# A pooled-attention and gated-MLP kernel: k's second half pooled into both partition halves, third unit's scores ahead of v's pooling, ten small matmuls left out

## The chip, the cores and the metric

One Trainium2 chip, one core. The metric is the device time of one execution in microseconds (us). Engines are called as in the profile: PE (TensorE matmuls), PEld (its weight loads), DVE (VectorE), ACT (ScalarE), POOL (GpSimd), SP (SyncE).

## What is computed

Attention over pooled keys and values, then a two-layer network with a cosine gate. Inputs are float32, the output is [4608, 512] float32.

```python
batch, n_heads, seq, head_dim = (8, 8, 576, 64)
pool = 8; Sp = S // pool            # 72
k_p = k.reshape(B, H, Sp, pool, D).mean(axis=3)
v_p = v.reshape(B, H, Sp, pool, D).mean(axis=3)
scores = (1 / sqrt(D)) * q @ k_p.T  # per batch and head: 576 x 72
attn = softmax(scores)
x = (attn @ v_p) -> [4608, 512]     # tokens x (heads, head_dim)
h = x @ w_in                        # w_in 512 x 2048
out = (h * cos(h)) @ w_out          # w_out 2048 x 512
```

## The kernel before

The 4608 tokens are worked through in nine chunks of 512 (`t` from 0 to 8). Each chunk goes up (lines 350 and 357 to 360: matmuls with `w_in`, a cosine on ACT, a product on DVE into `g_sb`) and down (line 363 or 369: matmuls with `w_out`). The attention of the next batch is threaded between a chunk's down matmuls at places written out by hand. Everything is ordered by hand (`manual_schedule`): each engine runs its instructions in the order in which the program issues them, and waits on semaphores where it needs another engine's or a DMA's result.

Batch 0 has nothing to hide behind. Its attention is a prologue (lines 401 to 544), and this is where the change is. It runs in this order.

- Ten matmuls of one column each (line 406) and nine `warm_up` matmuls of 128x512 on a constant (line 492) run on PE before any data is there.
- SP's queue fetches the first half of k and q of batch 0 (heads 0 to 3, line 416); POOL's queue fetches the second half of k (line 92), of q (line 437) and both halves of v (line 92), and then the weights `w_in` and `w_out` in many parts (lines 137 and 142), all one after another. ACT and DVE cast the first half of k and q to bf16 (`first_k`, `first_q`).
- `pool_k_pairs(b, bank, pj, ...)` pools k of one pair of heads on PE (line 184): nine accumulating matmuls, one for each row `t`, with k as the weights (128 rows, 64 columns) and the constant matrix `groups` as the moving operand (144 columns: 72 pooled positions for each of the pair's two heads). The result stands in PSUM on 64 partitions; its `put` casts it into `kk` for both halves of the partitions (line 189), for each half by a copy of its own. `kk` holds pooled k twice since q, once transposed, may stand on either half.
- `q_transpose_mm` transposes blocks of q on PE (line 236) and copies them into `qT` (line 237).
- `scores(b, u, pair)` computes the scores of a unit, here 256 tokens by 4 heads: four matmuls (line 259) and an exp on ACT into `ex` (line 269). Batch 0 has four such units, `us[0]` to `us[3]`, ordered by heads, so that units 0 and 1 need pairs 0 and 1 of k and q, units 2 and 3 pairs 2 and 3. (A rest of 64 tokens comes with a later batch.)
- `sums_mm` (line 288) sums the exponentials with matmuls against a constant; ACT turns the sums into reciprocals with Ln and Exp (lines 523, 524, 303, 304).
- `pool_v_mm(b, pair, j0, j1)` pools v (line 198): 18 matmuls of 64 rows and 128 columns; its `put` copies to `vz` on DVE (line 202).
- `values_mm` (line 297) multiplies exponentials with pooled v, and `x_mul` (line 311) multiplies by the reciprocal on DVE into `xT`, which the up matmuls (line 350) read. The first eight up matmuls need heads 0 to 3 alone (units 0 and 1); the next need units 2 and 3.

PSUM is eight banks of 512 float32 per partition: `banks` are three pairs (called `one`, `two`, `three` in the prologue) and `obanks` two single ones.

Of the kernel before, what the change touches and what calls it, by code (L numbers as in the profile page):

```python
# [19 lines left out]
def kernel(  # L20
# [9 lines left out]
    nc = tc.nc  # L30
    B, H, S, D = q.shape
    Sp = S // POOL
# [7 lines left out]
    ROW = S // 64  # L40
# [27 lines left out]
    kk = [wpool.tile([128, H, SpA], BF16, name=f"kk{i}") for i in range(3)]  # L68
# [8 lines left out]
    def own(b):  # L77
        return b % 2 if b else 2

    banks = [psum.tile([128, 2, 512], FP32, name=f"bank{i}") for i in range(3)]  # L80
    obanks = [psum.tile([128, 512], FP32, name=f"obank{i}") for i in range(2)]
# [4 lines left out]
    staged, flat = {}, {}  # L86

    def even_view(src, b, j0=0, j1=KCH):
        return src[b, 2 * j0:2 * j1].rearrange("(j a) (p t) d -> (a p) j (t d)", a=2, t=ROW)
# [64 lines left out]
    half = (slice(0, 64), slice(64, 128))  # L154

    def v_part(b):
        return vz[own(b)][:, :, 0:4:3, :]
# [19 lines left out]
            s = s.rearrange("p (j a) t d -> p j a t d", a=2)  # L177
            add(out=v_part(b)[:, h0 // 2:h1 // 2], in0=s[..., 0, :], in1=s[..., 1, :], op=ADD)  # L178

    def pool_k_pairs(b, bank, pj):  # L180

        ps = bank[half[0], 0:2 * Sp]
        for t in range(ROW):
            nc.tensor.matmul(ps, lhsT=staged["k", b][:, pj, t, :], rhs=groups[:, t].rearrange("p a n -> p (a n)"),
                             start=(t == 0), stop=(t == ROW - 1))

        def put(copy):
            for rows in half:
                copy(out=kk[own(b)][rows, 2 * pj:2 * pj + 2, 0:Sp], in_=ps.rearrange("p (a n) -> p a n", a=2))

        return put

    def pool_v_mm(b, pair, j0, j1):
        vb = staged["v", b]
        n = (j1 - j0) * D
        for t in range(ROW):
            for hp, rows in enumerate(half):
                nc.tensor.matmul(pair[:Sp, hp, 0:n], lhsT=groups[rows, t, hp, :], rhs=vb[rows, j0:j1, t, :],
                                 start=(t == 0), stop=(t == ROW - 1))

        def put():
            nc.vector.tensor_copy(out=v_part(b)[:, j0:j1],
                                  in_=pair[:Sp, :, 0:n].rearrange("p a (j d) -> p j a d", d=D))

        return put
# [24 lines left out]
    def q_transpose_mm(b, bank, g0, g1):  # L230

        if ("qT", b) not in att:
            qT_tile(b)
        ps = bank.bitcast(BF16)[:, 0:(g1 - g0) * 128].rearrange("p (g n) -> p g n", n=128)
        for g in range(g0, g1):
            nc.tensor.matmul(ps[:, g - g0, :], flat[b][:, g * 128:(g + 1) * 128], identity, is_transpose=True)
        return lambda copy: copy(out=att["qT", b][:, g0:g1, :], in_=ps)  # L237
# [6 lines left out]
    def scores(b, u, pair):  # L244
        scores_mm(b, u, pair)
        scores_exp(b, u, pair)

    def scores_mm(b, u, pair):
        (c0, n), (h0, nh) = u

        for i in [i + 2 * a for k in range(0, nh, 4) for i in (k, k + 1) for a in range(2)]:
            bank, c = divmod(ex_col(u, i), nh * n // 2)
            pj, hp = divmod(h0 + i, 2)
            g, r = divmod(ROW * pj + ORDER[c0 // 64], 2)
            qT = att["qT", b]
            if (b, u) == (0, REST):
                (g, r), qT = divmod(pj, 2), att["qT", B - 1][:, QB:]
            ps = pair[bank][:Sp, c:c + n] if isinstance(pair, tuple) else pair[:Sp, bank, c:c + n]
            nc.tensor.matmul(ps.rearrange("p (g n) -> p g n", n=64),  # L259
                             lhsT=kk[own(b)][half[r], h0 + i, 0:Sp],  # L260
                             rhs=qT[half[r], g:g + n // 64, hp * 64:hp * 64 + 64])

    def scores_exp(b, u, pair):
        (c0, n), (h0, nh) = u
        ex = ex_rest[own(b)] if u == REST else asb.tile([Sp, 4 * 256], BF16, name="ex", tag="ex", bufs=EX)
        w = nh * n // 2
        for src, c, m in ([(pair[:Sp, :, 0:w], 0, 2)] if not isinstance(pair, tuple) else
                          [(bank[:Sp, 0:w].unsqueeze(1), a * w, 1) for a, bank in enumerate(pair)]):
            nc.scalar.activation(out=ex[:, c:c + m * w].rearrange("p (a n) -> p a n", a=m), in_=src,  # L269
                                 func=ACTF.Exp, scale=scale / POOL)  # L270
        att["ex", b, u] = ex
# [130 lines left out]
    kv_even_tiles(0)  # L402
    q_tile(0)
    one_of = nc.const_aps.tensor(1.0, [128, 1], BF16)
    for i in range(10):
        nc.tensor.matmul(obanks[0][0:1, 0:1], lhsT=one_of, rhs=one_of)
    nc.vector.memset(staged["q", 0][:, :, ROW - 1], 0.0)
    exp_tables()
    groups = consts.tile([128, ROW, 2, Sp], BF16, name="groups")
# [5 lines left out]
    for i, (src, n) in enumerate(((k, ROW * D), (q, (ROW - 1) * D))):  # L415
        nc.sync.dma_start(out=first[:, i].rearrange("p (j n) -> p j n", j=2)[:, :, 0:n],
                          in_=even_view(src, 0, 0, 2)[:, :, 0:n])
# [5 lines left out]
    def first_q(copy, j):  # L423
        n = ROW * D
        copy(out=staged["q", 0][:, j, 0:ROW - 1].rearrange("p t d -> p (t d)"), in_=first[:, 1, j * n:j * n + n - D])
# [4 lines left out]
    for rows in half:  # L430
# [7 lines left out]
                        in_=even_view(q, 0, 2, 4)[:, :, 0:(ROW - 1) * D])  # L438
# [50 lines left out]
    def warm_up(n, bank):  # L489

        for i in range(n):
            nc.tensor.matmul(bank, lhsT=one_of.to_broadcast([128, 128]), rhs=one_of.to_broadcast([128, 512]))

    vec, act = nc.vector.tensor_copy, nc.scalar.copy
    us = BY_HEADS
# [3 lines left out]

    one, two, three = banks  # L500
    warm_up(9, two[:, 0, :])
    puts = [pool_k_pairs(0, obanks[i], i) for i in range(2)]
    first_q(act, 0)
    first_q(vec, 1)
    puts[0](vec)
# [3 lines left out]
    warm_up(1, two[:, 0, :])  # L509
    scores(0, us[0], one)  # L510
    scores(0, us[1], two)
    puts = [pool_k_pairs(0, obanks[i], 2 + i) for i in range(2)]
    for put in puts:
        put(vec)
    s01 = one[:, 0, 256:512], two[:, 0, 0:256]
    sums_mm(0, us[0], s01[0].unsqueeze(1))
    puts = q_transpose_mm(0, three[:, 0, :], 9, 14), q_transpose_mm(0, three[:, 1, :], 14, 18)
# [4 lines left out]
    for i in range(2):  # L522
        nc.scalar.activation(out=inv01[:, 256 * i:256 * i + 256], in_=s01[i], func=ACTF.Ln)
    nc.scalar.activation(out=inv01, in_=inv01, func=ACTF.Exp, scale=-1.0)
    put = pool_v_mm(0, one[:, :, 0:128], 0, 2)
    scores(0, us[2], three)
    scores(0, us[3], two)
    put()
    for i in range(2):
# [24 lines left out]
    for t in range(NT):  # L554
        b = t + 1
        bk = [banks[1], banks[0], banks[2]] if t == 1 else banks
        for fp in range(FFCH // 2):
# [5 lines left out]
            if t == 0:  # L563
                if fp == 6:
                    puts = q_transpose_mm(1, obanks[0], 0, 5), q_transpose_mm(1, obanks[1], 5, 9)
# [67 lines left out]
        elif b < B:  # L633
            us = BY_TOKENS
# [94 lines left out]
```

## Time and profile before

| | |
|---|---|
| median of 3 runs | 290.07 us (289.63 to 290.08) |
| profiled execution | 289.4 us |
| its span, first to last instruction | 287.5 us |
| PE busy | 282.1 us (98%), 1962 matmuls |
| DVE, ACT, POOL busy | 172.6, 144.2, 147.3 us |
| down matmuls, line 363 | 379 ns each by the profile |
| copies of `kk`, line 189, on DVE | 283 to 302 ns each |

Times in the profile's views are microseconds from the start of the span. In a timeline a row is: start, busy time, engine, line, operation, what is written and read, count, and in brackets the idle time of the engine before it and what ended that. Matmuls are pipelined: one that takes 379 ns may be followed by the next after 216, and the time of a group goes to its last end. The span is the time from the first instruction to the last; 1.9 us of the profiled execution's own time lie around it.

### The profile page before, as it was taken

How to read it: one execution, taken by the hardware profiler on the slowest of the kernel's cores; microseconds unless marked ns; L12 is line 12 of the kernel's file. 1: busy time of each engine (PE TensorE's matmuls, PEld its weight loads, DVE VectorE, ACT ScalarE, POOL GpSimd, SP SyncE). 2: the span in 40 equal slices, each digit the busy share in tenths (PEclk: the TensorE clock that was granted, in tenths of full speed). 3: DMA queues.
4: the chain of work that ended last, by engine and by line, in shares of the span. 5: the costliest groups of instructions: out<-in, count | busy, mean ns of one | idle time of the engine just before them, and what ended most of it. 6: DMA issues, size and time to landing. Idle time of an engine off the chain costs nothing.

```text
span 287.5 us, 4892 instructions
## 1 busy us (share of the span) xinstructions
PE 282.1 (98%) x1962; PEld 147.6 (51%) x1962; DVE 172.6 (60%) x233; ACT 144.2 (50%) x145; POOL 147.3 (51%) x126
## 2 busy tenths in 40 slices
PE   8899999999999999999999999999999999999995
PEld 4655544555555545555555545554555554445444
DVE  7557677766657555757475826582766657216623
ACT  6886626686067804690369226841676066006500
POOL 8546937999944895469647963699000000000010
PEclk9999999999999999999999999999999999999999
DMA  7999999899877959696879566976604620131033
GB/s 199 196 205 210 206 206 193 178 156 207 138 150 109 180 116 175 81 192 105 176 102 181 111 134 116 174 144 138 121 1 56 128 55 2 42 81 23 2 72 75
DMA packets 57878, 36.92 MB, mean 128 GB/s; under 512 B 37184, under 2 KB 51712, under 8 KB 57856
## 3 DMA queue, kind: packets, MB, share of 16 engines
q0 software_dynamic: 17728, 18.06, 39.2%
q1 hardware_dynamic: 39888, 18.43, 32.6%
q8 instruction: 15, 0.25, 0.4%
q10 hardware_dynamic: 240, 0.13, 0.2%
q14 instruction: 7, 0.06, 0.1%
HBM read 36.70 MB, written 9.44 MB: 160 GB/s over the span
## 4 chain that ended last, share of the span: by engine, by line
PE 93%; DMA 3%; ACT 1%; POOL 1%; DVE 0%; issue 0%; POOLq 0%
PE bank L350 43%; PE obank L363 27%; PE bank L363 8%; PE obank L369 5%; PE bank L259 3%; DMA kv_st<-in_v_dram 3%; PE bank L328 3%; PE bank L369 2%; PE bank L395 1%; ACT ex L269 1%; PE bank L297 0%; POOL kv_st L92 0%; PE bank L288 0%; ACT inv_h L304 0%; DVE xT L311 0%
## 5 line engine op out<-in xcount | busy, mean ns | idle before, releaser
L357 ACT ACTIVATE cos<-bank,half_pi 128x1024 f32<-128x1024 f32 x72 | 80.3, 1117 | 115.5 <-PE bank L350 115.5
L350 PE MATMUL bank<-xT,w_in_sb 128*128 128x512 bf16 x576 | 126.1, 379 | 0.1
L360 DVE TENSOR_TENSOR g_sb<-bank,cos 128x1024 bf16<-128x1024 f32 x72 | 88.1, 1224 | 48.6 <-ACT cos L357 48.5
L350 PEld LDWEIGHTS <-w_in_sb 128*128 128x128 bf16 x576 | 65.1, 113 | 59.3 <-issue 0.6
L363 PE MATMUL obank<-w_out_sb,g_sb 128*128 128x512 bf16 x360 | 84.2, 379 | 0.0
L363 PEld LDWEIGHTS <-g_sb 128*128 128x128 bf16 x460 | 41.8, 97 | 45.6 <-issue 2.0
L168 POOL TENSOR_TENSOR kv_st<-kv_st 72x2048 f32<-72x2048 bf16 (+1 forms) x13 | 50.4, 3876 | 15.6 <-DMA kv_st<-in_k_dram 15.6
L387 POOL DMA_DIRECT2D out_dram<-o_sb x2 | 1.1, 558 | 74.0 <-DVE o_sb L380 74.0
L269 ACT ACTIVATE ex<-bank 72x1024 bf16<-72x1024 f32 x32 | 30.4, 1019 | 4.8 <-PE bank L259 4.8
L171 POOL TENSOR_TENSOR kv_st<-kv_st 72x1024 f32<-72x1024 f32 (+1 forms) x13 | 29.2, 2250 | 0.9
L380 DVE COPY o_sb<-obank 128x512 f32<-128x512 f32 x19 | 13.0, 690 | 24.9 <-PE obank L363 21.9
L363 PE MATMUL bank<-w_out_sb,g_sb 128*128 128x512 bf16 x100 | 27.0, 379 | 0.0
L332 DVE TENSOR_TENSOR x_r<-bank,inv_r 128x512 bf16<-128x512 f32 (+1 forms) x32 | 22.0, 689 | 1.1
L369 PE MATMUL obank<-w_out_sb,g_sb 64*128 64x512 bf16 x144 | 18.2, 376 | 0.0
L175 POOL TENSOR_TENSOR kp<-kv_st 72x512 bf16<-72x512 f32 (+1 forms) x14 | 16.1, 1168 | 0.5
L369 PEld LDWEIGHTS <-g_sb 64*128 64x128 bf16 x200 | 9.9, 94 | 7.5
L259 PE MATMUL bank<-qT,kk 64*72 64x256 bf16 (+1 forms) x192 | 12.9, 247 | 0.4 <-DVE qT L237 0.4
L259 PEld LDWEIGHTS <-kk 64*72 64x72 bf16 x192 | 8.3, 111 | 7.6 <-issue 2.8
L328 PEld LDWEIGHTS <-ex 72*128 72x128 bf16 x192 | 8.8, 97 | 6.2 <-ACT ex L269 1.9
L123 POOL DMA_DIRECT2D kv_st<-in_v_dram x15 | 9.6, 654 | 4.2 <-DVE vz L178 4.2
L329 DVE RECIPROCAL inv_r<-bank 128x8 f32<-128x8 f32 (+1 forms) x32 | 6.5, 203 | 8.6 <-PE bank L328 7.9
L550 POOL COPY gate<-kk 1x1 bf16<-1x1 bf16 x5 | 0.9, 177 | 20.6 <-DMA kk<-kp 20.6
(89 smaller groups left out, 178.5 us busy)
## 6 DMA issues: line engine op xcount, KB each, us to landing
out_dram<-o_sb SPq DMA_DIRECT2D x68, 128.0 KB, 2.4
q_b<-in_q_dram POOLq DMA_DIRECT2D x6, 576.0 KB, 8.2
kv_st<-in_k_dram POOLq DMA_DIRECT2D x6, 512.0 KB, 5.9
kv_st<-in_v_dram POOLq DMA_DIRECT2D x6, 512.0 KB, 10.3
w_in_sb<-in_moe_w_in_dram POOLq DMA_DIRECT2D x8, 256.0 KB, 10.5
w_out_sb<-in_moe_w_out_dram POOLq DMA_DIRECT2D x8, 256.0 KB, 10.1
kv_st<-in_k_dram POOLq DMA_DIRECT2D x3, 288.0 KB, 10.3
g_sb<-in_k_dram SPq DMA_DIRECT2D x1, 576.0 KB, 3.7
```

Source lines behind the costliest of these rows:

```text
L168: add(out=s, in0=x[:, :, 0:4, :], in1=x[:, :, 4:8, :], op=ADD)
L171: add(out=s[:, :, 0:2, :], in0=s[:, :, 0:2, :], in1=s[:, :, 2:4, :], op=ADD)
L175: add(out=kp[:, h0:h1, slot, :], in0=s[:, :, 0, :], in1=s[:, :, 1, :], op=ADD)
L259: nc.tensor.matmul(ps.rearrange("p (g n) -> p g n", n=64), lhsT=kk[own(b)][half[r], h0 + i, 0:Sp], rhs=qT[half[r], g:g + n // 64, hp * 64: ...
L269: nc.scalar.activation(out=ex[:, c:c + m * w].rearrange("p (a n) -> p a n", a=m), in_=src, func=ACTF.Exp, scale=scale / POOL)
L328: nc.tensor.matmul(out[:, o0:o0 + D + 1], lhsT=ex[:, c:c + 128], rhs=v1)
L332: nc.vector.tensor_mul(out=x[:m].rearrange("p e h d -> p h e d"), in0=vals, in1=scale_of)
L350: nc.tensor.matmul(h[:, j, :], lhsT=w_in_cols(ki, fc), rhs=xT[:, ki % 2, ki // 2, t * TILE:(t + 1) * TILE], start=(ki == 0), stop=(ki == K ...
L357: nc.scalar.activation(out=cos, in_=h, func=ACTF.Sin, bias=half_pi[:, :1])
L360: nc.vector.tensor_mul(out=g_sb[:, 2 * fp:2 * fp + 2, :], in0=h, in1=cos)
L363: nc.tensor.matmul(o, lhsT=g_sb[:, fc, ms * 128:(ms + 1) * 128], rhs=w_out_sb[fc // 4][:, fc % 4, :], start=(fc == 0), stop=(fc == FFCH - 1))
L369: nc.tensor.matmul(ps, lhsT=g_sb[rows, fc, ms * 128:(ms + 1) * 128], rhs=w_out_sb[fc // 4][rows, fc % 4, :], start=start, stop=stop)
```

## The change

Three edits, all in batch 0's prologue.

- `pool_k_pairs` takes a flag `twice`. Without it (pairs 0 and 1) it does what it did. With it (pairs 2 and 3) every matmul is issued twice, once for each half of PSUM's partitions, and `put` copies all 128 partitions at once: 36 matmuls in place of 18, two copies in place of four.
- The ten matmuls of one column at the start are left out.
- The third unit's scores (matmuls and exp) are issued before the pooling of v's first half instead of after it.

```diff
-    def pool_k_pairs(b, bank, pj):
-
-        ps = bank[half[0], 0:2 * Sp]
+    def pool_k_pairs(b, bank, pj, twice):
+
+        ps = bank[:, 0:2 * Sp]
         for t in range(ROW):
-            nc.tensor.matmul(ps, lhsT=staged["k", b][:, pj, t, :], rhs=groups[:, t].rearrange("p a n -> p (a n)"),
-                             start=(t == 0), stop=(t == ROW - 1))
+            for rows in half[:1 + twice]:
+                nc.tensor.matmul(ps[rows], lhsT=staged["k", b][:, pj, t, :],
+                                 rhs=groups[:, t].rearrange("p a n -> p (a n)"), start=(t == 0), stop=(t == ROW - 1))
 
         def put(copy):
-            for rows in half:
-                copy(out=kk[own(b)][rows, 2 * pj:2 * pj + 2, 0:Sp], in_=ps.rearrange("p (a n) -> p a n", a=2))
+            to, src = kk[own(b)][:, 2 * pj:2 * pj + 2, 0:Sp], ps.rearrange("p (a n) -> p a n", a=2)
+            if twice:
+                copy(out=to, in_=src)
+            else:
+                for rows in half:
+                    copy(out=to[rows], in_=src[half[0]])
...
     one_of = nc.const_aps.tensor(1.0, [128, 1], BF16)
-    for i in range(10):
-        nc.tensor.matmul(obanks[0][0:1, 0:1], lhsT=one_of, rhs=one_of)
...
     warm_up(9, two[:, 0, :])
-    puts = [pool_k_pairs(0, obanks[i], i) for i in range(2)]
+    puts = [pool_k_pairs(0, obanks[i], i, False) for i in range(2)]
...
     scores(0, us[0], one)
     scores(0, us[1], two)
-    puts = [pool_k_pairs(0, obanks[i], 2 + i) for i in range(2)]
+    puts = [pool_k_pairs(0, obanks[i], 2 + i, True) for i in range(2)]
     for put in puts:
         put(vec)
...
     nc.scalar.activation(out=inv01, in_=inv01, func=ACTF.Exp, scale=-1.0)
+    scores(0, us[2], three)
     put = pool_v_mm(0, one[:, :, 0:128], 0, 2)
-    scores(0, us[2], three)
     scores(0, us[3], two)
     put()
```

## The prediction

> **What bounds the kernel now.** I read the page's chain first, to learn where a change in the prologue is felt, then the chain's pieces up to 17 us, and then the timelines of PE, DVE and ACT over the same stretch.
>
> ```profile
> PE 93%; DMA 3%; ACT 1%; POOL 1%; DVE 0%; issue 0%; POOLq 0%
> ```
>
> Nearly all of the span is TensorE, and from 16.76 us on its records show no gap over 0.1 us up to the end. So whatever moves the matmul that starts at 16.76 moves the end by as much, and the question is confined to the 16.76 us before it. There the chain reads (start, length, what):
>
> ```profile
> 3.07 8.04 DMA kv_st<-in_v_dram
> 11.11 0.04 issue
> 11.15 0.69 PE bank L198 x18
> 11.85 0.24 PE bank L259 x4
> 12.09 0.02 issue
> 12.11 1.94 ACT ex L269 x2
> ```
>
> The first half of v lands at 11.11, its pooling (L198) runs at once, and only behind that come the third unit's scores (L259) and their exp. The timelines (start, length, engine and line) show what stands beside this:
>
> ```profile
> 0.79 0.39 PE L406 MATMUL obank<-const-bfloat16-1.0 128*1 128x1 bf16 x10 [0.79 <-PEq L713]
> 1.11 4.02 PE L492 MATMUL bank<-const-bfloat16-1.0 128*128 128x512 bf16 x9
> 5.24 1.41 PE L184 MATMUL obank<-groups,kv_st 128*64 128x144 bf16 x18
> ...
> 8.44 1.31 PE L184 MATMUL obank<-groups,kv_st 128*64 128x144 bf16 x18
> 9.69 0.29 PE L288 MATMUL bank<-ex,ones 72*32 72x256 bf16 x4
> ...
> 11.15 0.69 PE L198 MATMUL bank<-kv_st,groups 64*72 64x128 bf16 x18 [0.34 <-DMA kv_st<-in_v_dram]
> 11.68 0.60 PE L259 MATMUL bank<-qT,kk 64*72 64x256 bf16 x8
> 12.43 0.62 PE L297 MATMUL obank<-ex,vz 72*32 72x256 bf16 x16
> 12.98 0.69 PE L198 MATMUL bank<-kv_st,groups 64*72 64x128 bf16 x18
> 14.79 2.56 PE L350 MATMUL bank<-xT,w_in_sb 128*128 128x512 bf16 x10
> ...
> 9.23 1.26 DVE L189 CAST kk<-obank 64x144 bf16<-64x144 f32 x4 [1.44 <-PE obank L184]
> 10.69 0.82 DVE L237 COPY qT<-bank 128x640 bf16<-128x640 bf16 x2 [0.20 <-PE bank L236]
> 11.96 0.42 DVE L202 CAST vz<-bank 72x256 bf16<-72x256 f32 x1 [0.44 <-ACT inv L524]
> 14.06 0.68 DVE L311 TENSOR_TENSOR xT<-obank,inv 128x512 bf16<-128x512 f32 x1
> ```
>
> Two things matter. The transposed q that the third unit reads is copied by DVE until 10.69 + 0.82 = 11.51, so its scores, started at 11.68, waited for v by hardly 0.1 us: the pooling filled PE time that was otherwise empty. And the first up-projection matmul (L350) starts at 14.79, 0.05 after DVE's second product (14.06 + 0.68), which descends from v's pooling: pooling, copy L202, values L297, pooling of v's second half, copy, product.
>
> **k's second half.** 18 matmuls more (36 for 18) and two copies fewer. The row of 18 takes 1.31 with a last matmul of 0.23 (the line's own view: 226 ns), so one follows the other after (1.31 - 0.23) / 17 = 0.064. What a second matmul costs that writes partitions 64 to 127 is not in the trace. Lower bound: nothing, because the four sums matmuls at 9.69, each to 32 columns of its own, take 0.29 together where one takes 0.28; likewise 16 values matmuls take 0.62. Upper bound: 18 x 0.064 = 1.15, no overlap at all. A gain is excluded, the first nine pairs being the old work. I take 0, since both near rows write column groups side by side with weights loaded between. [...]
>
> The copies: four of 0.30 (L189, 9.23 to 10.49) become two of 128x144. Their price is by elements per partition (64x144 takes 0.30; I take the same; the six of that shape on DVE run from 283 to 302 ns). DVE is free at about 10.14, not 10.49. That is worth nothing: the next DVE instruction, the first q copy, waited for PE anyway (idle 0.20 to 10.69, released by the transposes), and all of them are done only at 10.59. The cover is that wait; without it the saving would be 0.35.
>
> **The ten tiny matmuls.** They take 0.79 to 1.11, so the nine warm-ups start 0.32 earlier and end near 4.81 in place of 5.13. Pooling still waits for ACT's cast of k at 5.24, itself behind a DMA: gain 0. The cost to bound is the clock. The windows view grants 1.00 throughout, but durations tell: warm-ups take 634 ns at the start and 379 ns at 7.10, and the pooling row holds a longest of 327 against a median of 226, its first two being slow. So full speed came about 5.5, and PE's hole before it grows from 0.11 to 0.43. I take 0 (a short hole in a long busy stretch); the other end is a rival below.
>
> **The order.** Only PE's queue changes: pooling and scores carry no DMA, ACT had the third exp next and DVE the copy L202 in any case. Third unit's scores: their first matmul goes 0.05 after the q copies (the handover seen at 12.43 and 14.79), 11.51 + 0.05 = 11.56 for 11.68. The exp started 0.43 after it, so 11.99 for 12.11; ACT is free from 11.28 + 0.63 = 11.91, so it does not bind. Gain on ACT: 0.12.
>
> v's pooling, first half: now queued behind those four matmuls, which wait for DVE while v lies ready. They occupy two steps of 0.11 ((0.60 - 0.27) / 3, in pairs), so pooling starts at 11.78 for 11.15: later by 0.63. Less a slow first pair of 0.02 that a running PE does not have: 0.61. Everything in its descent keeps its spacing: copy L202 12.57, values 13.04, second pooling 13.59 (its v landed at 12.58), second product ending 15.35, first up-projection 15.40 for 14.79. The copies and products wait on nothing later: the last scores end near 12.7, before the exp on ACT wants them at 12.9.
>
> The other arm: the last two sums stand behind the second pooling, the first at 13.61 + 0.61 = 14.22 and the second 0.11 on, 14.33 for 14.09. ACT's logarithms and exps follow 0.24 later, and the last product ends at 16.71 + 0.24 = 16.95. Before, that product set 16.76: the first eight up-projections took 14.79 + 8 x 0.216 = 16.52, and PE stood 0.24 idle. Now they end at 15.40 + 1.73 = 17.13, after the product. So the stall goes, and what is late is PE itself: 17.13 - 16.76 = +0.37, and that passes to the end.
>
> Sum: 0 + 0 + 0 + 0.37. The profiled execution took 289.4 (span 287.5, 1.9 around it), so 289.8 by it. The median of the runs, 290.07, stands 0.7 above it; by that, 290.4 us, 0.13% slower, inside the 0.2% (0.58 us) that a measurement of this kernel can tell from no change.
>
> **Rivals.**
>
> Full speed comes late (slower). If the larger hole spoils the stretch of work that raises the clock, the first pooling and the nine transposes stay at half rate: 1.31 - 0.23 = 1.08 more, of which 0.12 was slow already, and 0.68 - 0.22 = 0.46 more: 1.42. Scores, second pooling (its k landed at 8.40, just in time for 8.44) and all behind move with it: 0.37 + 1.42 = +1.8, 291.9. It decides from the point where 0.43 of idle time is too much and 0.11 is not. For it: speed came only 4.4 us after the warm-ups' start. Against: the warm-ups start earlier too. [...]
>
> The column halves do not overlap (slower): +1.15 on everything from 9.69 on, 0.37 + 1.15 = +1.5, 291.6. Against it: the sums and values rows. [...]
>
> v lands late (about level). Before, all shifts with the landing; after, nothing does until it passes 11.74. Break-even is 11.11 + 0.37 = 11.48, the most is 0.37 - 0.63 = -0.26, 289.8. The landing is the end of a queue of transfers at a full DMA; this trace alone shows it.
>
> Full speed comes sooner (faster): if in ordinary runs the clock rises late and the earlier warm-ups bring it forward over the pooling, 1.42 - 0.37 = -1.05, 289.0. For it: the times, profiled one included, differ by 0.7. Against: here only two matmuls were slow.
>
> The reorder doing nothing at all, v landing at its break-even, lies inside the forecast's own range.
>
> **How the numbers follow.** Forecast 53%, its own range 290.0 to 290.7 (an earlier v makes it up to +0.46, for then the old scores would have gained their 0.1 too); 11 of the 53 lie past 290.65. Late speed 22%, no overlap 11%, late v 6%, speed sooner 8%. Slower by over 0.2%: 11 + 22 + 11 = 44%. Within: 42 + 6 = 48%. Faster: 8%. The range runs from 289.7 to 291.7: out are the sooner speed and half of the late speed, 19%.
>
> **What would show it.** Right: warm-ups from about 0.8; 36 matmuls at L184's later row in about 1.3; two kk copies of 128x144 ending near 10.15 with q's copies still at 10.7; third scores at 11.56, exp at 12.0, v's pooling only at 11.8, first up-projection at 15.4 with no idle time after its eighth matmul, the next at 17.1. Wrong: a pooling row near 2.4; first-pooling matmuls of 290 ns or more beyond the first few; v's landing past 11.5; or an up-projection that starts before 15.2.

## The result and the profile after

The change makes the kernel slower by 0.2%: 290.11 us (median of 21 runs, 289.9 to 290.8) against 289.46 us before (21 runs, 289.24 to 290.08), a ratio of 1.0023 with a 95% interval of 1.0016 to 1.003. The profiled execution took 289.99 us with a span of 287.8 us; before it was 289.4 and 287.5. So of 0.6 us between the two executions, 0.3 lie in the span and 0.3 outside it (2.2 us around the span in place of 1.9). Over all runs it is much the same: the span's median is 288.0 and what lies around it 2.15, against 287.6 and 1.90 for the kernel before in the 33 runs timed beside the first experiments.

The span first. The chain of the kernel after, in order of time (start, length, what; "issue" is time in which the profile shows nothing that the engine waits for), from the pooling of k's second half on:

```profile
8.43 1.25 PE obank L185 x36
9.68 0.22 PE bank L293 x4
9.90 0.62 PE bank L241 x9
...
10.62 0.83 DVE qT L242 x2
11.45 0.04 issue
11.49 0.41 PE bank L264 x4
11.90 0.52 PE bank L203 x18
...
14.75 0.40 PE obank L302 x8
15.15 0.22 PE bank L302 x8
15.37 0.35 PE bank L355
```

v's landing is no longer in the chain. In its place stand q's copies (L242) and, behind them, the third unit's scores (L264) and only then v's pooling (L203). (Lines have moved by up to five: L185 was L184, L203 was L198, L264 was L259, L355 was L350.) The timelines of PE and DVE show the same from the engines' side (start, length, engine, line):

```profile
0.79 3.76 PE L495 MATMUL bank<-const-bfloat16-1.0 128*128 128x512 bf16 x9 [0.79 <-PEq L716]
5.28 1.31 PE L185 MATMUL obank<-groups,kv_st 128*64 128x144 bf16 x18 [0.72 <-ACT kv_st L424]
8.36 1.32 PE L185 MATMUL obank<-groups,kv_st 128*64 128x144 bf16 x36
11.49 0.41 PE L264 MATMUL bank<-qT,kk 64*72 64x256 bf16 x4 [0.76 <-DVE qT L242]
11.71 0.69 PE L203 MATMUL bank<-kv_st,groups 64*72 64x128 bf16 x18
15.35 3.40 PE L355 MATMUL bank<-xT,w_in_sb 128*128 128x512 bf16 x14
...
9.16 0.31 DVE L191 CAST kk<-obank 128x144 bf16<-128x144 f32 x1 [1.44 <-PE obank L185]
9.80 0.31 DVE L191 CAST kk<-obank 128x144 bf16<-128x144 f32 x1 [0.33 <-PE obank L185]
10.62 0.82 DVE L242 COPY qT<-bank 128x640 bf16<-128x640 bf16 x2 [0.51 <-PE bank L241]
```

PE stood 0.76 us waiting for q's copies, with v in place since 10.98, and began to pool v at 11.71, before at 11.15. The first up-projection starts at 15.35 for 14.79. ACT's exp did start earlier, at 11.94 for 12.11, and that bought nothing.

What reaches the end of the span is the ninth up-projection. Its rows, before and after (a window that opens behind the eighth):

```profile
16.76 3.61 PE L350 MATMUL bank<-xT,w_in_sb 128*128 128x512 bf16 x16
...
17.07 3.18 PE L355 MATMUL bank<-xT,w_in_sb 128*128 128x512 bf16 x14
```

Before, it came 0.46 us after the start of the eighth (16.30), with 0.25 of idle time in between; after, it comes 0.22 behind it (16.85), with none. So of the 0.56 us that the first up-projection lost, the idle time absorbed 0.25, and 0.31 are left, about what the span lost (287.8 for 287.5).

### The profile page after: what moved, and what is told of

Its sections match the earlier page's. It is cut to its first block, busy times and chain, and to the rows that moved or that the text cites. A ratio compares the mean times of both kernels' runs of the same rounds, so it can differ in the third digit from the quotient of the medians.

```text
span 287.8 us, 4873 instructions
## 1 busy us (share of the span) xinstructions
PE 278.4 (97%) x1937; PEld 147.1 (51%) x1970; DVE 172.2 (60%) x231; ACT 144.2 (50%) x145; POOL 147.4 (51%) x126
## 4 chain that ended last, share of the span: by engine, by line
PE 92%; DVE 3%; ACT 2%; DMA 1%; issue 1%; DVEq 0%
PE bank L355 41%; PE obank L368 26%; PE bank L368 7%; PE obank L374 5%; PE bank L264 3%; PE bank L333 3%; PE bank L374 2%; DVE g_sb L365 2%; ACT cos L362 2%; DMA g_sb<-in_k_dram 1%; PE bank L400 1%; PE obank L185 1%; PE bank L241 1%; DVE qT L242 0%; PE bank L302 0%
## 5 line engine op out<-in xcount | busy, mean ns | idle before, releaser
L355 PE MATMUL bank<-xT,w_in_sb 128*128 128x512 bf16 x564 | 125.4, 379 | 0.6
L355 PEld LDWEIGHTS <-w_in_sb 128*128 128x128 bf16 x576 | 65.1, 113 | 59.1 <-issue 0.2
L368 PE MATMUL obank<-w_out_sb,g_sb 128*128 128x512 bf16 x347 | 82.7, 379 | 0.4
L368 PE MATMUL bank<-w_out_sb,g_sb 128*128 128x512 bf16 x92 | 25.4, 379 | 1.2 <-issue 1.1
L264 PE MATMUL bank<-qT,kk 64*72 64x256 bf16 (+1 forms) x192 | 13.2, 247 | 1.7 <-DVE qT L242 1.1
L264 PEld LDWEIGHTS <-kk 64*72 64x72 bf16 x192 | 8.4, 111 | 8.5 <-issue 3.5
## 6 DMA issues: line engine op xcount, KB each, us to landing
kv_st<-in_k_dram POOLq DMA_DIRECT2D x3, 288.0 KB, 10.5
```

What stands on the lines that cost most here:

```text
L264: nc.tensor.matmul(ps.rearrange("p (g n) -> p g n", n=64), lhsT=kk[own(b)][half[r], h0 + i, 0:Sp], rhs=qT[half[r], g:g + n // 64, hp * 64: ...
L355: nc.tensor.matmul(h[:, j, :], lhsT=w_in_cols(ki, fc), rhs=xT[:, ki % 2, ki // 2, t * TILE:(t + 1) * TILE], start=(ki == 0), stop=(ki == K ...
L368: nc.tensor.matmul(o, lhsT=g_sb[:, fc, ms * 128:(ms + 1) * 128], rhs=w_out_sb[fc // 4][:, fc % 4, :], start=(fc == 0), stop=(fc == FFCH - 1))
```

## Experiments

Each kernel was timed in five rounds beside the kernel before; spans and the time around them are medians over the runs. The kernel before was timed anew beside each of three groups of experiments: medians 289.46, 289.48 and 289.55 us, with 1.90 or 1.91 around the span each time.

**The order alone.** The last hunk of the change on the kernel before:

```diff
+    scores(0, us[2], three)
     put = pool_v_mm(0, one[:, :, 0:128], 0, 2)
-    scores(0, us[2], three)
```

> The kernel before with the third unit's scores moved ahead of the pooling of v's first half, nothing else. Theory (v's pooling waits behind scores that wait for q's copies): pooling of v starts near 11.7 to 11.8 in place of 11.15, the first up-projection matmul near 15.3 to 15.4 in place of 14.79, the eighth ends without idle time; span about +0.35 us, time +0.3 to +0.5 us, nearly the whole of the change's +0.65. Rival (the extra loss comes from the other two edits): +0.1 us or less.

Measured: 289.77 us against 289.46, ratio 1.0014 (1.0005 to 1.0023); span 287.9 against 287.6, 1.88 around it. Its PE timeline:

```profile
10.38 0.29 PE L288 MATMUL bank<-ex,ones 72*32 72x256 bf16 x4
11.43 0.41 PE L259 MATMUL bank<-qT,kk 64*72 64x256 bf16 x4 [0.76 <-DVE qT L237]
11.64 0.70 PE L198 MATMUL bank<-kv_st,groups 64*72 64x128 bf16 x18
15.28 1.02 PE L350 MATMUL bank<-xT,w_in_sb 128*128 128x512 bf16 x3
```

The same wait, the same late pooling, the same late up-projection as in the whole change: the order makes the loss of the span. But 0.3 is about half of 0.65 and not nearly the whole, as I had expected: the other two edits must account for more than the 0.1 that I had granted them.

**The ten small matmuls alone.** On the kernel before:

```diff
-    for i in range(10):
-        nc.tensor.matmul(obanks[0][0:1, 0:1], lhsT=one_of, rhs=one_of)
```

> The kernel before without the ten one-column matmuls, nothing else. Theory: 0 (within 0.15 us), since the first pooling still starts when ACT's cast of k is done, near 5.25; the nine warm-ups end some 0.3 us earlier. Rival (the longer hole between warm-ups and pooling makes full speed come late in part of the runs): +0.3 us or more in the median, a wider spread of the runs, first pooling row near 2.4 in place of 1.3 to 1.4.

Measured: 289.40 against 289.46, ratio 0.9995 (0.9987 to 1.0004); runs from 289.17 to 289.81, span 287.5. No effect that can be told from none, and no wider spread: in the profiled execution PE stood 0.46 us ahead of the first pooling, in the kernel before 0.11, and the pooling took 1.31 us, before 1.41.

**The doubled pooling alone.** `pool_k_pairs` as after, the order and the ten matmuls as before.

> The kernel before with k's second half pooled into both partition halves and two copies in place of four, nothing else. Theory: 0 (within 0.1 us): 36 matmuls in 1.3 us as 18 before, DVE idle 0.35 us longer ahead of q's copies, which still start near 10.7. Rival (the second column half costs time): pooling row near 2.4, +1.1 us.

Measured: 289.68 against 289.46, ratio 1.0012 (1.0003 to 1.0021). Its span is that of the kernel before, 287.6; around it lie 2.18 us, before 1.90. The timelines:

```profile
8.57 1.32 PE L185 MATMUL obank<-groups,kv_st 128*64 128x144 bf16 x36
9.81 0.29 PE L293 MATMUL bank<-ex,ones 72*32 72x256 bf16 x4
...
10.00 0.31 DVE L191 CAST kk<-obank 128x144 bf16<-128x144 f32 x1 [0.33 <-PE obank L185]
10.82 0.82 DVE L242 COPY qT<-bank 128x640 bf16<-128x640 bf16 x2 [0.51 <-PE bank L241]
```

36 matmuls take 1.32, where 18 took 1.31; DVE waits 0.51 ahead of q's copies where it waited 0.20. Inside the span the theory holds. The time was expected within 0.1 us of the kernel before and is 0.2 above it; what was lost lies outside the first and last instruction.

**The scores without their wait.** In the kernel after, the third unit's scores read the first unit's operands again, and the later transposes of q go to other banks:

```diff
-    puts = q_transpose_mm(0, three[:, 0, :], 9, 14), q_transpose_mm(0, three[:, 1, :], 14, 18)
+    puts = q_transpose_mm(0, obanks[0], 9, 14), q_transpose_mm(0, obanks[1], 14, 18)
...
-    scores(0, us[2], three)
+    scores_mm(0, us[0], three)
+    scores_exp(0, us[2], three)
```

> The kernel after, but the third unit's score matmuls read the first unit's q and k again (so the third unit's scores are not the reference's), and the two later groups of q's transposes go to the single banks, so that these scores wait neither for q's copies nor for their bank. Theory: the scores run near 10.7, their exp starts when ACT is free, near 11.9; v's pooling runs on landing, near 11.1; first up-projection near 14.75, the ninth near 16.6: about 0.5 us faster than the kernel after and 0.1 to 0.2 faster than the kernel before in its span. Rival (the order itself costs, not the wait): v's pooling still late, no gain over the kernel after.

Measured: 289.50 us, ratio to before 1.0007 (0.9994 to 1.0019); span 287.4, 2.02 around it. From its timelines of PE and ACT:

```profile
10.86 0.41 PE L264 MATMUL bank<-qT,kk 64*72 64x256 bf16 x4
11.10 0.67 PE L203 MATMUL bank<-kv_st,groups 64*72 64x128 bf16 x18
14.71 5.47 PE L355 MATMUL bank<-xT,w_in_sb 128*128 128x512 bf16 x23
...
11.93 1.91 ACT L274 ACTIVATE ex<-bank 72x1024 bf16<-72x1024 f32 x2
```

Order and all as in the kernel after, but no wait: the scores fit in ahead of v, the pooling runs at 11.10, the span is 0.6 us below the kernel after and 0.2 below the kernel before. The order is harmless; scores that wait for DVE at the head of PE's queue are not. (This run takes away the wait for the copies and the wait for their bank together; the next one takes away part of it with the right operands.)

**q's transposes in other banks, scores honest.** Only the first two lines of the diff above, on the kernel after.

> The kernel after with the two later groups of q's transposes in the two single banks in place of the two halves of the third pair of banks; all else as after. Theory (the loss in the span is that v's pooling waits behind scores that wait for q's copies): DVE starts the first of these copies after five transposes instead of nine, 0.2 us earlier; scores and v's pooling move up by 0.2, first up-projection near 15.15, span 0.2 us below the kernel after. Rival (v's landing or ACT sets the end): span as after.

Measured: 289.67 us, ratio to before 1.0003 (0.9995 to 1.0012); span 287.6, that is 0.4 below the kernel after and level with the kernel before; 2.04 around it. DVE and PE:

```profile
10.29 0.82 DVE L242 COPY qT<-obank 128x640 bf16<-128x640 bf16 x2 [0.22 <-PE obank L241]
...
10.84 0.71 PE L264 MATMUL bank<-qT,kk 64*72 64x256 bf16 x4
11.31 0.68 PE L203 MATMUL bank<-kv_st,groups 64*72 64x128 bf16 x17
14.98 5.34 PE L355 MATMUL bank<-xT,w_in_sb 128*128 128x512 bf16 x24
```

With the two groups in tiles of their own, the first copy no longer waits for all nine transposes and starts 0.33 earlier; the pooling follows at 11.31 for 11.71, the up-projection at 14.98 for 15.35. That is nearly twice the gain that was expected: I had counted 0.2 for the copy.

**The order undone, the rest kept.** The kernel after with the two lines swapped back.

> The kernel after with the order undone (v's pooling ahead of the third unit's scores again), the doubled pooling and the missing ten matmuls kept. Theory: span as the kernel before (within 0.1 us), 2.1 to 2.2 outside, so +0.1 to +0.25 us against before: the order is the whole loss of the span, the doubled pooling the loss outside it. Rival (the edits act on one another): span 0.2 us or more off the kernel before's.

Measured: 289.73 against 289.48, ratio 1.0004 (0.9994 to 1.0013); span 287.6 as before, 2.14 around it. The split in span and time around it stands: the span's loss comes from the order, the time around it from what is left of the change. The total itself cannot be told from that of the kernel before.

**What lies outside the span.** First guess: the length of PE's instruction list. Ten one-column matmuls more, where PE waits:

```diff
     warm_up(1, two[:, 0, :])
+    for i in range(10):
+        nc.tensor.matmul(two[0:1, 0, 0:1], lhsT=one_of, rhs=one_of)
```

> The kernel before with ten more one-column matmuls, right after the single warm-up, where TensorE waits 0.5 us for q's copy anyway: 20 PE instructions more (matmuls and weight loads), 3946 in place of 3926, nothing else. The runs with the doubled pooling (3942 and 3962 PE instructions) had 2.0 to 2.2 us outside the span, those without it (3906 and 3926) 1.9. Theory (the length of PE's instruction list sets this): span as before, 2.1 to 2.2 outside, median +0.2 to +0.3 us. Rival (something in the doubled pooling itself, or chance): 1.9 outside, time as before.

Measured: 289.41 against 289.48, ratio 1.0 (0.9991 to 1.0009), span 287.5, 1.89 around it. The guess falls. Then half of the doubling:

```diff
-    puts = [pool_k_pairs(0, obanks[i], 2 + i, True) for i in range(2)]
+    puts = [pool_k_pairs(0, obanks[i], 2 + i, i == 0) for i in range(2)]
```

> The kernel after, but of k's second half only pair 2 is pooled into both partition halves; pair 3 as in the kernel before (18 matmuls and weight loads, 18 PE instructions fewer: 3924). Theory of PE's list length: span as the kernel after (about 287.9 to 288.0 median), 1.9 outside, median about 0.25 us below the kernel after, some +0.35 to +0.4 against before. Rival (doubled pooling itself): outside 2.0 to 2.1, time as the kernel after.

Measured: 289.66, ratio 1.0009 (1.0 to 1.0018); span 287.9, but 1.77 around it, less than before. Not PE's list, for that would have given 1.9, and not the doubling by itself either. What did go with it in all runs so far was the number of DVE instructions in the trace (waits counted): 316, 317, 318 and 319 gave 2.02 to 2.04, 2.14 to 2.18, 1.77 and 1.88 to 1.90. (The two kernels with 316 also have one ACT instruction fewer, 242 for 243.) So four kernels changed that number, by one-element memsets where DVE waits:

```diff
     puts[1](act)
+    for i in range(2):
+        nc.vector.memset(gate, 0.0)
```

On the kernel after, two of them:

> The kernel after with two one-element DVE memsets more, right behind the first pooling's copies, where DVE waits 0.3 us for PE anyway. So far the time outside the span went with the number of DVE instructions in the trace and with nothing else: 319 gave 1.89 us (four kernels), 318 gave 1.77, 317 gave 2.14 to 2.16 (three), 316 gave 2.02 (two). Theory (DVE's instruction count, in a saw-tooth that repeats every four): 319 again, 1.89 outside, span as after, so 0.25 us below the kernel after. Rival (the doubled pooling itself): outside 2.15, time as after.

Measured: 289.83, ratio 1.0012 (1.0004 to 1.0021); span 288.1, 1.79 around it. The trace holds 318 DVE instructions, not 319, since a separate wait fell away, and 1.79 is what 318 gave in one_twice. With the doubled pooling untouched, two needless memsets take 0.36 us off the time around the span (2.15 to 1.79), and the loss against the kernel before timed beside it falls from 0.65 to 0.28. What is left is the order's: the span is 288.1 against 287.7.

On the kernel before, two and one:

> The kernel before with the same two memsets more: 321 DVE instructions, nothing of the change in it. Theory of DVE's count: 2.15 outside the span, span as before, +0.25 us. Rival (doubled pooling, or fewer DVE instructions being worse): outside 1.9, time as before.

> The kernel before with one such memset more: 320 DVE instructions. Theory of DVE's count with a period of four: 2.02 outside the span, span as before, +0.12 us. Rival: outside 1.9, time as before.

Measured: 289.39 and 289.69 against 289.55, ratios 0.9997 (0.9988 to 1.0005) and 1.0001 (0.9991 to 1.001); 1.77 and 1.75 around the span, with 320 DVE instructions in both traces. Expected were 2.15 and 2.02: the saw-tooth falls.

And on the kernel before without its ten matmuls, three:

> The kernel before without the ten one-column matmuls and with three such memsets more: 322 DVE instructions. Theory of DVE's count: 1.77 outside the span; with the span of no_tiny (0 to 0.1 us below before) 0.1 to 0.2 us faster than the kernel before, the best of all. Rival: outside 1.9, time as the kernel before.

Measured: 289.58 against 289.55, ratio 1.0003 (0.9994 to 1.0011); 321 instructions and not the expected 322, 1.78 around a span of 287.8. The 1.78 is near the 1.77 expected, but the gain of 0.1 to 0.2 us did not come. So this is no faster version, and none of the kernels here beats the kernel before beyond its interval.

What is shown: the kernel's time outside the span moves between 1.75 and 2.18 us; it is above 2.0 in every kernel that pools both later pairs doubly, with two DVE copies fewer, and has no memset added; two instructions given back to DVE, with the doubling kept, put it below that of the kernel before. That the two saved copies alone raise it is argued and not shown: every kernel with 316 or 317 DVE instructions has the doubled pooling too, and none was run that has the pooling as before and fewer than 319. By which rule, a threshold at 318, alignment or something else, is open: 316 and 317 were high, 318 to 321 low, and no kernel with more or fewer was run.

The traces hold one more sign of it. They show a last transfer of 8 KB on an instruction queue (q14) that starts after the last instruction of the span: 0.3 us after it with 321 DVE instructions, 0.6 with 320, 1.1 with 319 or 318, 1.6 with 317, 1.7 to 2.0 with 316. With 319 it is 1.1 also where PE has 20 instructions more or 20 fewer. So something behind the span does go with the length of DVE's list; but the time around the span does not rise in the same order (319 lies above 318, 316 below 317), so this transfer does not give the rule.

## Why the prediction was right, and the term it lacked

The measured time, 290.11, lies in the likeliest case's own range, and the mechanism of the order is the one that ran. That the number fits is in part luck: measured, the change costs 0.65 us, above the most that the prediction's terms gave (+0.46), and a base that was too high made up for it. (The upper end of the case's range, 290.7, has no term behind it either: 290.07 + 0.46 is 290.53.) By its steps:

- **Order, +0.37.** The span moved by 0.3 in the profiled pair and 0.4 in the medians, and no_q_wait shows that it was for the reason given. The scores started at 11.49 (11.56 forecast), v's pooling at 11.71 (11.78), the first up-projection at 15.35 (15.40), 0.56 later than before for 0.61, and the ninth at 17.07 (17.13) without the idle time; a few hundredths less each, with PE's work from 6.5 to 11 us some 0.07 earlier in that execution. The base execution was itself a little late: its first pooling took 1.41. Where the traces show 1.31, the ninth starts at 16.57 to 16.64 in the old order (no_tiny, before_memset_2, no_tiny_memset_3) and at 17.00 to 17.25 in the new one (order_only, after, one_twice, after_memset_2), which fits the 0.4 of the medians better than the profiled pair does. The larger chance, 48%, went to a change of less than 0.2%; the median came out at 0.23%, just past that edge.
- **k's second half, 0 on PE.** Right: 36 matmuls, each with a weight load of 0.11 (after, L185, median 110 ns), took 1.32 where 18 took 1.31. The upper bound, 1.15 more, came in none of the rows of 36.
- **The copies, worth nothing.** Right for the reason given: q's first copy started at 10.62 with 0.51 of idle time before it. The copies take 0.31 each, not 0.30. But "nothing" was the step that failed: with this edit the time outside the span is 0.25 us longer (twice_only 2.18, after 2.15, before 1.90), and two one-element DVE instructions more take that away again (after_memset_2 1.79). The sum took the 1.9 around the span as fixed. It is not, and no row of the span shows it.
- **The ten matmuls, 0.** Right: -0.06 with an interval on both sides of none.
- **The base.** The forecast went from a median of three runs, 290.07. With 21 runs it is 289.46, 0.6 lower, nearly the 289.4 of the profiled execution. The predicted 290.4 is near 290.11 because a base too high by 0.6 and a difference too small by 0.28 (0.37 for 0.65) partly cancel.

The rivals: late speed as an effect of the change is refuted by no_tiny and by the pooling row of 1.31 in the kernel after, behind 0.72 of idle time. Nor did the earlier warm-ups bring a gain by sooner speed: no_tiny is level with the kernel before (ratio 0.9995). That the work ahead of the pooling raises the speed, and a hole spoils it, was my supposition; no run shows what sets the time: the pooling took 1.31 behind those 0.72 us and 2.06 behind 0.04 (before_memset_1). A slow first pooling does occur as scatter between executions, with the change's edits and without. Two profiled executions, of old_order and of before_memset_1, had it:

```profile
5.34 1.98 PE L185 MATMUL obank<-groups,kv_st 128*64 128x144 bf16 x18 [0.55 <-ACT kv_st L424]
```

```profile
5.17 2.06 PE L184 MATMUL obank<-groups,kv_st 128*64 128x144 bf16 x18
```

Each has the first pooling about 0.7 us longer than the 1.31 of the fastest (half of the 1.42 that the rival put down: the nine transposes behind it took 0.68 as elsewhere), and spans of 288.1 and 288.3 where the least span of the same kernel is 287.3 and 287.4. That scatter is wide enough to make the median of three runs a poor base. No overlap of the column halves is refuted by the rows of 36: 1.32 in after, twice_only, no_q_wait, q_banks and old_order. v landing past 11.48, where the rival begins, was seen in one trace of 14 (before_memset_1, at 11.54, where all of PE ran some 0.7 late); in the others it lands between 10.69 and 11.20, in the kernel after at 10.98. v held up its pooling most in the kernel before, by 0.34, until 11.15.

## What to carry to other kernels

Before moving work ahead of a wait on an engine whose order is fixed by hand, ask which of the two operands is ready first: here v was ready half a microsecond before q (10.98 for 11.45 in the kernel after), and the pooling had been filling an empty stretch. The slack at the end of a chain (here 0.25 us of idle PE ahead of the ninth up-projection) covers only its own length of a shift of 0.56; the rest reaches the end. When a change is worth a few tenths of a microsecond, compare the time around the span as well as the span, and use enough runs of the kernel before to place its median.

## What the runs showed of the hardware that I had not expected

- The time outside the span went with DVE's list of instructions: 2.02 to 2.18 us with 316 or 317 of them, 1.75 to 1.90 with 318 to 321. Two one-element memsets, nothing else, took it from 2.15 to 1.79 in the kernel after and from 1.90 to 1.77 in the kernel before. Twenty PE instructions more moved it by no more than 0.02.
- The matmuls' speed rose at a time that differed from one execution to the next. In the kernel before, a warm-up of 128x512 took 634 ns at the start and 379 at 7.10; in the kernel after, the ninth, at 4.16, took 394. With the same PE work ahead of it the first pooling of 18 took between 1.31 us (before_memset_2) and 2.06 (before_memset_1). The granted clock reads 1.00 in every window of the prologue in the traces of before and after.
- Two matmuls with the same weights and the same moving operand, written to the two halves of PSUM's partitions, cost no more than one: 36 in 1.32 us (after) for 18 in 1.31 (before).
